# Fetching weight words earlier and chunk inputs later in the first steps of a fused linear-attention and FFN kernel

## The chip, the cores and the metric

The kernel runs on one NeuronCore of a Trainium2 chip. The metric is the device time of one execution in microseconds (us); lower is better. The engines are named as in the profile: PE is the matrix engine (PEld its weight loads), DVE the vector engine, ACT the scalar engine, POOL the GpSimd engine, and SP the engine whose queue issues most of the DMA transfers.

## The reference, cut to what matters

```python
# attention: B=4, H=8, S=768, D=48, all float32
for t in range(S):
    state = alpha[:, :, t, :, None] * state + einsum('bhd,bhe->bhde', k[:, :, t], v[:, :, t])
    y[:, :, t] = einsum('bhd,bhde->bhe', q[:, :, t], state)
# bridge: y (B,H,S,D) -> x (B*S, H*D) = (3072, 384)
# FFN: w1, w2 (384, 1024), w3 (1024, 1024), w_out (1024, 384), all float64 in memory
a = x @ w1
b = x @ w2
h = a * b @ w3
out = h @ w_out          # (3072, 384)
```

The gated recurrence of every head feeds a multiplicative FFN. The FFN weights arrive as float64 words, and the kernel itself turns them into float32.

## The kernel before, in words

**Chunks and steps.** The sequence of each batch is cut into chunks of 128 rows, six to a batch, so there are `N` = 24 chunks over the four batches. The main loop (line 599) runs `n` from 0 to 24; one round is called a step. In step n the kernel computes the score matrices of chunk n (`scores`, PE line 364, masked on DVE line 367), finishes the attention output of chunk n-1 (`attend_state` line 384, `attend` line 390, copied out by ACT line 394), forms the new state (`outer`, line 336) and transposes q and k of chunk n+1 (`transposed`, PE line 324, copied by ACT line 326). It also prepares later chunks: `decayed(n + 2)` (DVE line 302) multiplies k and q by the decay factors, `logs(n + 4)` (ACT line 271) takes logarithms of alpha, and `decays(n + 3)` (PE lines 286 and 289, ACT lines 292 and 293) sums them and takes exponentials. Chunk inputs come by the SP queue: alpha by `load_a` (line 132), k and q by `load_kq` (lines 138 and 139), v by `load_v` (line 144). Each such load is 192 KB in rows of 192 bytes. At the head of step n the kernel before issues v of chunk n+3, alpha of chunk n+5 and k, q of chunk n+4 (`AHEAD` is 4).

**Weight units.** The w1 and w2 matrices are cut into twelve units of 128 x 512 words of 8 bytes (512 KB each). `load_gates` is a generator: its first call issues the transfer (line 192), and four more calls do the conversion. The first of these works out mantissa and exponent (DVE lines 201 and 204, ACT lines 200 and 205), the second combines them (DVE lines 207, 208 and 210), the third makes the rounded high part (ACT line 217), and the fourth makes the low part (DVE line 219). `fetch(ahead)` issues transfers until `ahead` units are under way, and `convert(steps, ahead)` makes so many calls. For the first six units, which hold the columns that the first four tiles of a gate use, the third part of the split comes from two PE matmuls and an ACT copy (`third`, lines 232 to 234).

**Gates.** Three chunks make a group of 384 rows. When a group's three outputs have been written to DRAM (`store`, line 261), `load_x` (line 406) reads them back transposed as `xT`, `split_x` splits them into three parts (ACT line 412, DVE lines 413 and 414), and `gate` multiplies them with w1 and w2. A gate of one tile of columns has two pieces of nine PE matmuls each (line 420); after six of the nine, ACT line 429 scales the partial sum, and DVE line 431 adds the rest. During the main loop the gates of the first tiles fill PE: `run(...)` takes pieces from the deque `fill`, and `pieces` says how many a step takes. Group g begins in step 6 + 4g of the kernel before, and its pieces are taken 3, 3 and 2 in the three following steps.

**After the loop.** The remaining gates are put in a list `todo` (line 668), in which the folding of w3 with w_out is interleaved (`fold`, PE line 522 and line 420 with `w3T`). When the folding is done, its memory is closed, a new pool is opened, and `load_ab` (line 543) and `split_ab` (ACT line 550, DVE lines 551 and 552) bring back the products for the last stage, `project` (line 420 with `w3o`).

**What sets the order.** The order of the instructions on each engine is fixed at build time. The program's order and the calls of `after_marks`, which put instructions behind a named earlier one, decide it. SP issues its transfers in that order as well.

Of the kernel before, what the change touches and what calls it, by code (L numbers as in the profile page):

```python
# [10 lines left out]
FP32 = mybir.dt.float32  # L11
# [5 lines left out]
ALU = mybir.AluOpType  # L17
# [3 lines left out]
P = 4096.0  # L21
# [27 lines left out]
def kernel(  # L49
# [12 lines left out]
    nc = tc.nc  # L62
# [5 lines left out]
    N = B * NCH  # L68
    NP = H // 2
    DP = 64  # L70
    KM = DM // C
    KF = DF // C
# [4 lines left out]
    AHEAD = 4  # L77
# [28 lines left out]
    st, mark = {}, {}  # L106

    def after_marks(*names):
        stack = ExitStack()
        for x in names:  # L110
            stack.enter_context(tc.issue_after(mark[x]))
        return stack
# [12 lines left out]
    def rows(src, n):  # L125
        b, c = divmod(n, NCH)
        return src[b, :, ds(c * C, C), :].rearrange("h p d -> p h d")

    def load_a(n):
        if n < N:  # L130
            st["a", n] = inp.tile([C, H, D], FP32, tag="ac", name="ac")
            nc.sync.dma_start(out=st["a", n], in_=rows(alpha, n))  # L132

    def load_kq(n):
        if n >= N:
            return
        st["kq", n] = inp.tile([C, 2, H, D], FP32, tag="kq", name="kq")
        nc.sync.dma_start(out=st["kq", n][:, 0], in_=rows(k, n))  # L138
        nc.sync.dma_start(out=st["kq", n][:, 1], in_=rows(q, n))  # L139

    def load_v(n):
        if n < N:
            st["v", n] = vs[n % len(vs)]
            nc.sync.dma_start(out=st["v", n][:, :, 0:D], in_=rows(v, n))
# [69 lines left out]
    def load_gates(i, kk, half):  # L214
        w = yield from to_fp32(None, (moe_w1, moe_w2)[i][ds(kk * C, C), ds(half * CW, CW)])
        h, l, m = (w12[half][:, x, i, kk, :] for x in range(3))
        nc.scalar.activation(h, w, AF.Copy, scale=(1.0 - 2.0 ** -13) / P)
        yield
        nc.vector.scalar_tensor_tensor(l, h.bitcast(FP32), -P, w, op0=ALU.mult, op1=ALU.add)
        if half:  # L220
            nc.vector.scalar_tensor_tensor(m, h.bitcast(FP32), P + 1.0, w, op0=ALU.mult, op1=ALU.subtract)
        else:
            thirds.append((m, h, l))

    weights, begun, thirds = deque(), deque(), deque()

    def third(count):

# [7 lines left out]
    def fetch(ahead=3):  # L236
        while weights and len(begun) < ahead:
            begun.append(weights.popleft())
            next(begun[-1])

    def convert(steps, ahead=3):

        for _ in range(steps):
            fetch(ahead)
            if not begun:
                return
            x = begun.popleft()
            try:
                next(x)
                begun.appendleft(x)  # L250
            except StopIteration:
                pass
# [27 lines left out]
    def decays(n):  # L280
        if n >= N:
            return
        lc = bank()[:, 0:DM]
        la = st.pop(("la", n))
        if n < LATE:
            nc.tensor.matmul(lc, sums[:, n % 2].bitcast(FP32), la, start=True, stop=True)  # L286
        else:
            for i in range(2):
                nc.tensor.matmul(lc, sums[:, n % 2], la[:, i], start=(i == 0), stop=(i == 1))  # L289

        e = st["e", n] = work.tile([C, 2, DM], FP32, tag="e", name="e", bufs=3)
        nc.scalar.activation(e[:, 0], lc, AF.Exp, scale=-1.0)
        mark["e", n] = nc.scalar.activation(e[:, 1], lc, AF.Exp).ins  # L293
        if n in ends:
            nc.gpsimd.dma_start(out=ends[n][0:1], in_=e[0:1, 0])
        if n + 1 in ends:
            nc.gpsimd.dma_start(out=ends[n + 1][1:2], in_=e[C - 1:C, 1])
        load_ends(n)
# [109 lines left out]
    def split_x(g, i):  # L408
        x = st.pop(("xT", g))
        t = tr[i].tile([C, 3, KM, TG], FP32R, tag="x3", name="x3")  # L410
        st["x3", g] = t
        nc.scalar.activation(t[:, 0], x, AF.Copy, scale=1.0 - 2.0 ** -13)
        nc.vector.tensor_sub(t[:, 1], x, t[:, 0].bitcast(FP32))
        mark["x3"] = nc.vector.scalar_tensor_tensor(t[:, 2], t[:, 0].bitcast(FP32), -1.0 - 1.0 / P, x,
                                                    op0=ALU.mult, op1=ALU.add).ins
# [73 lines left out]
    def gate(g, f):  # L489
        yield from (late_gate if late else early_gate)(g, f)  # L490
# [71 lines left out]
    fill = deque()  # L562
# [11 lines left out]
    FH = CW // C  # L574
# [9 lines left out]
        logs(1)  # L584
    decays(1)
    fetch(1)
    load_v(1)
    load_kq(2)
    load_a(3)
    decayed(1)  # L590
    load_v(2)
    load_kq(3)
    load_a(4)


    begin = {4 + 4 * g: (g, range(FH if g < 4 else KF)) for g in range(5)}
    loads = {8: 1, 11: 2, 15: 3, 19: 4}

    for n in range(N + 1):
        store()  # L600
        if n in loads:
            load_x(loads[n])
        load_v(n + AHEAD - 1)
        load_a(n + 5)
        load_kq(n + AHEAD)
        if n:
            attend_state(n - 1)
        if n < N:
            scores(n)
        transposed(n + 1)  # L610
        if n - 2 in begin:
            g, tiles = begin[n - 2]
            with after_marks(("ms", n), ("qkT", n + 1)):
                split_x(g, 0)
            fill.extend(gate(g, f) for f in tiles)
        pieces = (0, 3, 3, 2)[(n - 6) % 4] if n > 5 else 0
        if n == 0:
            with after_marks(("qkT", 0)):
                logs(2)
            decays(2)  # L620
            with after_marks(("e", 2)):
                logs(3)
        early, ready = n < 7, len(thirds)
        behind = after_marks(*[("qkT", n + 1)] * (n < N - 1), *[("qk", n + 1)] * early, *["x3"] * (n - 2 in begin))
        if n < N - 2:
            with behind:
                convert(2 if n == 0 else 1, 2 if n == 0 else 3 if n < 8 else 4)
        advance(n)
        if n:
            attend(n - 1)  # L630
        outer(n)
        third(ready)
        run(pieces > 0)
        if early:
            with after_marks(("qkT", n + 1), ("qk", n + 1)):
                convert(1)
        with after_marks(*[("ms", n)] * (n < 3)):
            decayed(n + 2)
        logs(n + 4)
        if n == 4:  # L640
            load_x(0)
        convert(early and n > 2)
        run(pieces > 1)
        decays(n + 3)
        if n < N - 2:
            convert(early or n % 3 == 0, 3 if n < 8 else 4)
        run(pieces > 2)
        if n == N - 3:
            while begun:
                convert(1)  # L650
            weights.extend(load_out(j) for j in range(KF))
            fetch(4)
# [91 lines left out]
```

## Time and profile before

| quantity | value |
|---|---|
| median of three runs | 480.21 us (478.72 to 480.35) |
| profiled execution, own time | 478.61 us |
| span of its instructions | 476.8 us |
| PE busy / weight loads busy | 458.3 us (96%) / 435.2 us (91%) |
| DVE / ACT / POOL busy | 356.3 us (75%) / 282.1 us (59%) / 73.1 us (15%) |
| moved by DMA | 80.29 MB, mean 168 GB/s |
| mean granted PE clock | 0.982 |

The profiled execution took 478.61 us, of which 1.8 us lie outside the span of its instructions; its time is 1.6 us below the median of the three runs. The page cuts the span into 40 equal slices of 11.9 us. A busy PE in it is not a PE at full speed: where the granted clock is half, the same matmuls count about twice the time.

### The profile page before, as it was taken

What the parts mean: (1) busy time and instruction counts of PE and PEld (TensorE: products, weight loads), DVE (VectorE), ACT (ScalarE), POOL (GpSimd) and SP (SyncE); (2) the same over time, 40 slices, a digit from 0 to 9 for tenths busy, and PEclk for the clock granted to TensorE, in tenths of its full rate; (3) what the DMA queues carried; (4) which work ended last, traced back from release to release, by engine and by line L of the source; (5) the groups of instructions that cost most, each with busy time, mean ns of one, the idle gap of its engine ahead of it and who ended that gap; (6) DMA issues with size and microseconds to landing.
All of it is one profiled execution on the core that took longest, in us unless ns stands there. A gap on an engine that the chain in (4) does not pass through costs nothing.

```text
span 476.8 us, 10002 instructions
## 1 busy us (share of the span) xinstructions
PE 458.3 (96%) x3836; PEld 435.2 (91%) x3836; DVE 356.3 (75%) x576; ACT 282.1 (59%) x556; POOL 73.1 (15%) x140
## 2 busy tenths in 40 slices
PE   4879899999999999999999999999999999999996
PEld 2658589899899999999999999999999999999996
DVE  2769888886988988999998888745642876666761
ACT  4667766866758555898876666644545433333330
POOL 3321231112302310212331101202010100000000
PEclk9888889999999999999999999999999999999999
DMA  9999999999999964657775333122105965555511
GB/s 171 178 200 220 241 211 212 229 234 211 197 216 206 210 202 133 200 170 234 242 216 209 109 124 100 50 84 90 44 36 157 261 189 169 164 170 172 177 51 49
DMA packets 153583, 80.29 MB, mean 168 GB/s; under 512 B 104480, under 2 KB 145568, under 8 KB 153536
## 3 DMA queue, kind: packets, MB, share of 16 engines
q1 hardware_dynamic: 148016, 65.22, 56.8%
q0 software_dynamic: 5520, 14.43, 9.5%
q8 instruction: 30, 0.49, 0.5%
q14 instruction: 17, 0.14, 0.1%
HBM read 57.58 MB, written 22.06 MB: 167 GB/s over the span
## 4 chain that ended last, share of the span: by engine, by line
PE 87%; DMA 5%; SPq 3%; DVE 2%; ACT 1%; issue 1%; DVEq 0%; ACTq 0%
PE bank L420 70%; PE bank L364 5%; PE bank L390 4%; DMA raw<-in_moe_w_dram 4%; PE bank L384 2%; PE bank L324 2%; SPq L139 2%; PE bank L336 1%; PE bank L522 1%; PE bank L289 1%; DMA ac<-in_alpha_dram 1%; SPq L138 1%; SPq L132 1%; PE bank L286 1%; DVE ms L367 0%
## 5 line engine op out<-in xcount | busy, mean ns | idle before, releaser
L420 PE MATMUL bank<-x,w 128*128 128x384 f32 x1152 | 210.9, 337 | 0.0
L420 PEld LDWEIGHTS bank<-x,w 128*128 128x128 f32 x1152 | 200.4, 188 | 1.3 <-issue 0.7
L420 PE MATMUL bank<-w3o,ab 128*128 128x384 f32 x576 | 100.2, 336 | 0.0
L420 PEld LDWEIGHTS bank<-w3o,ab 128*128 128x128 f32 x576 | 99.9, 188 | 0.0
L445 ACT ACTIVATE bank<-bank 128x384 f32<-128x384 f32 x98 | 46.7, 477 | 43.6 <-PE bank L420 43.3
L429 ACT ACTIVATE t<-bank 128x384 f32<-128x384 f32 x62 | 30.6, 494 | 62.3 <-PE bank L420 60.1
L495 POOL DMA_DIRECT2D abd<-ab x46 | 26.9, 584 | 132.8 <-DVE ab L481 125.2
L481 DVE TENSOR_TENSOR ab<-bank,r 128x384 f32<-128x384 f32 x45 | 24.9, 552 | 23.4 <-ACT bank L445 18.6
L551 DVE TENSOR_TENSOR ab<-abl,ab 128x1024 fp32r<-128x1024 f32 x24 | 29.4, 1224 | 13.6 <-ACT ab L550 13.5
L550 ACT ACTIVATE ab<-abl 128x1024 fp32r<-128x1024 f32 x24 | 25.5, 1061 | 20.9 <-PE bank L420 19.2
L326 ACT COPY qkT<-bank 128x512 f32<-128x512 f32 x48 | 26.1, 591 | 19.0 <-PE bank L324 19.0
L367 DVE TENSOR_TENSOR ms<-bank,keep 128x512 int32<-128x512 int32 x48 | 31.4, 683 | 7.8 <-PE bank L364 7.8
L420 PE MATMUL bank<-wo,w3T 128*128 128x384 f32 x192 | 35.9, 334 | 0.0
L420 PEld LDWEIGHTS bank<-wo,w3T 128*128 128x128 f32 x192 | 33.5, 188 | 0.0
L364 PEld LDWEIGHTS bank<-qkT 48*128 48x128 f32 x384 | 25.7, 204 | 7.0 <-issue 4.2
L431 DVE SCALAR_TENSOR_TENSOR o<-bank,t 128x384 f32<-128x384 f32 x24 | 13.4, 557 | 24.0 <-issue 15.6
L364 PE MATMUL bank<-qkT 48*128 48x128 f32 x384 | 30.7, 304 | 0.4 <-ACT qkT L326 0.4
L552 DVE SCALAR_TENSOR_TENSOR ab<-ab,abl 128x1024 fp32r<-128x1024 f32 x24 | 29.2, 1217 | 0.0
L302 DVE TENSOR_TENSOR qk<-kq,e 128x768 f32<-128x768 f32 x24 | 23.0, 958 | 8.2 <-ACT e L293 8.1
L390 PE MATMUL bank<-ms,v 128*64 128x128 f32 x384 | 28.3, 293 | 0.0
L205 ACT ACTIVATE power<-power,rebias 128x512 uint32<-128x512 uint32 (+1 forms) x36 | 25.1, 701 | 4.1 <-DVE power L204 3.8
L200 ACT ACTIVATE rest<-raw 128x512 f32<-128x512 uint32 (+1 forms) x36 | 23.3, 650 | 7.1 <-DMA raw<-in_moe_w_dram 7.1
(80 smaller groups left out, 573.3 us busy)
## 6 DMA issues: line engine op xcount, KB each, us to landing
raw<-in_moe_w_dram SPq DMA_DIRECT2D x28, 512.0 KB, 5.2
abl<-abd SPq DMA_DIRECT2D x24, 512.0 KB, 4.6
abd<-ab POOLq DMA_DIRECT2D x46, 192.0 KB, 3.1
xT<-xd POOLq DMA_DIRECT2D x9, 576.0 KB, 4.5
ac<-in_alpha_dram SPq DMA_DIRECT2D x24, 192.0 KB, 4.7
kq<-in_k_dram SPq DMA_DIRECT2D x24, 192.0 KB, 5.4
kq<-in_q_dram SPq DMA_DIRECT2D x24, 192.0 KB, 4.4
v<-in_v_dram SPq DMA_DIRECT2D x24, 192.0 KB, 5.0
```

Of the source, the lines that this page charges most:

```text
L205: nc.scalar.activation(power, power, AF.Relu, scale=2.0 ** 23, bias=rebias)
L326: mark["qkT", n] = nc.scalar.copy(qkT[:, :, :, ds(DP * half, DP)], tp[half]).ins
L364: nc.tensor.matmul(sc[i][:, j, :], qkT[r, 0, j, :], qkT[r, 1, j, :], start=True, stop=True)
L367: masked = nc.vector.tensor_tensor(ms[:, i].bitcast(I32), sc[i].bitcast(I32), keep_bc, op=ALU.bitwise_and)
L390: nc.tensor.matmul(to, vc[:, 2 * j + i, :], ms[:, i, j, :], start=(n % NCH == 0 and j % HP == 0), stop=(j % HP == HP - 1), skip_group_chec ...
L420: nc.tensor.matmul(p, w[part][i], x[part][i], start=start and part == parts[0] and i == 0, stop=stop and part == parts[-1] and i == n - 1, ...
L429: nc.scalar.activation(t, p1, AF.Copy, scale=(1.0 + 1.0 / P) * scale)
L445: nc.scalar.activation(p, p, AF.Copy, scale=1.0 + 1.0 / P)
L495: (nc.gpsimd if late else nc.sync).dma_start(out=abd[g][:, f, :], in_=ab)
L550: nc.scalar.activation(t[:, 0], ab, AF.Copy, scale=1.0 - 2.0 ** -13)
L551: nc.vector.tensor_sub(t[:, 1], ab, t[:, 0].bitcast(FP32))
L552: nc.vector.scalar_tensor_tensor(t[:, 2], t[:, 0].bitcast(FP32), -1.0 - 1.0 / P, ab, op0=ALU.mult, op1=ALU.add)
```

## The change: its parts and the diff

Before the loop, k, q and v of one chunk less are loaded, alpha of chunk 3 moves ahead of k and q of chunk 2, and a second weight unit is fetched. In steps 0 to 6, k and q are issued three chunks ahead and v two; step 6 issues two chunks of them, and from then on the distance is the old one. The number of units under way is written out per step in `raws`, and a `fetch` stands ahead of the k, q, v loads in steps 0 to 3. One more `convert` call is made in steps 1 and 2, and none of the extra ones in step 6, so that all 24 calls for the first six units are made by the end of step 5. The first group's `split_x` moves from step 6 to the end of step 5, behind the last low part of a unit (`mark["l"]`). Every later group begins a step sooner, and the pieces are taken 3, 3, 2, 0 beginning in step 6 rather than 0, 3, 3, 2. The `load_x` calls keep their steps. In the static order of the changed program one gate less is left for `todo`: 36 matmuls instead of 54 stand between the last fold's `w3T` matmuls and the first `w3o` matmuls.

```diff
--- before.py
+++ after.py
@@ -216,13 +216,14 @@
         h, l, m = (w12[half][:, x, i, kk, :] for x in range(3))
         nc.scalar.activation(h, w, AF.Copy, scale=(1.0 - 2.0 ** -13) / P)
         yield
-        nc.vector.scalar_tensor_tensor(l, h.bitcast(FP32), -P, w, op0=ALU.mult, op1=ALU.add)
+        mark["l"] = nc.vector.scalar_tensor_tensor(l, h.bitcast(FP32), -P, w, op0=ALU.mult, op1=ALU.add).ins
+        done.append((i, kk, half))
         if half:
             nc.vector.scalar_tensor_tensor(m, h.bitcast(FP32), P + 1.0, w, op0=ALU.mult, op1=ALU.subtract)
         else:
             thirds.append((m, h, l))
 
-    weights, begun, thirds = deque(), deque(), deque()
+    weights, begun, thirds, done = deque(), deque(), deque(), []
 
     def third(count):
 
@@ -584,47 +585,51 @@
         logs(1)
     decays(1)
     fetch(1)
+    load_a(3)
+    load_kq(2)
     load_v(1)
-    load_kq(2)
-    load_a(3)
     decayed(1)
-    load_v(2)
-    load_kq(3)
+    fetch(2)
     load_a(4)
 
 
-    begin = {4 + 4 * g: (g, range(FH if g < 4 else KF)) for g in range(5)}
+    FIRST = 6
+    begin = {FIRST - 3 + 4 * g: (g, range(FH if g < 4 else KF)) for g in range(5)}
     loads = {8: 1, 11: 2, 15: 3, 19: 4}
 
     for n in range(N + 1):
         store()
         if n in loads:
             load_x(loads[n])
-        load_v(n + AHEAD - 1)
         load_a(n + 5)
-        load_kq(n + AHEAD)
+        raws = (3, 3, 3, 3, 2, 2, 3, 3)[n] if n < 8 else 4
+        if n < FIRST - 2:
+            fetch(raws)
+        for m in (n + 3,) * (n <= FIRST) + (n + 4,) * (n >= FIRST):
+            load_kq(m)
+            load_v(m - 1)
         if n:
             attend_state(n - 1)
         if n < N:
             scores(n)
         transposed(n + 1)
-        if n - 2 in begin:
+        if n - 2 in begin and n > FIRST:
             g, tiles = begin[n - 2]
             with after_marks(("ms", n), ("qkT", n + 1)):
                 split_x(g, 0)
             fill.extend(gate(g, f) for f in tiles)
-        pieces = (0, 3, 3, 2)[(n - 6) % 4] if n > 5 else 0
+        pieces = (3, 3, 2, 0)[(n - FIRST) % 4] if n >= FIRST else 0
         if n == 0:
             with after_marks(("qkT", 0)):
                 logs(2)
             decays(2)
             with after_marks(("e", 2)):
                 logs(3)
-        early, ready = n < 7, len(thirds)
-        behind = after_marks(*[("qkT", n + 1)] * (n < N - 1), *[("qk", n + 1)] * early, *["x3"] * (n - 2 in begin))
+        early, ready = n < FIRST, len(thirds)
+        behind = after_marks(*[("qkT", n + 1)] * (n < N - 1), *[("qk", n + 1)] * early, *["x3"] * (n - 2 in begin and n > FIRST))
         if n < N - 2:
             with behind:
-                convert(2 if n == 0 else 1, 2 if n == 0 else 3 if n < 8 else 4)
+                convert(2 if n == 0 else 1, raws)
         advance(n)
         if n:
             attend(n - 1)
@@ -633,17 +638,23 @@
         run(pieces > 0)
         if early:
             with after_marks(("qkT", n + 1), ("qk", n + 1)):
-                convert(1)
+                convert(1, raws)
         with after_marks(*[("ms", n)] * (n < 3)):
             decayed(n + 2)
         logs(n + 4)
         if n == 4:
             load_x(0)
-        convert(early and n > 2)
+        convert(early and n > 0, raws)
         run(pieces > 1)
         decays(n + 3)
         if n < N - 2:
-            convert(early or n % 3 == 0, 3 if n < 8 else 4)
+            convert(early or n % 3 == 0, raws)
+        if n == FIRST - 1:
+            assert len(done) == 2 * KM
+            g, tiles = begin[n - 2]
+            with after_marks("l"):
+                split_x(g, 0)
+            fill.extend(gate(g, f) for f in tiles)
         run(pieces > 2)
         if n == N - 3:
             while begun:
```

## Prediction

> **What bounds the kernel now.** I began with the page's totals and its 40 slices, then read the chain of waits, the windows and the timeline of the first 90 us, and last the timeline where the final stage begins. By "step n is at t" I mean that its first matmuls on PE begin at t.
>
> ```profile
> PE 458.3 (96%) x3836; PEld 435.2 (91%) x3836; DVE 356.3 (75%) x576; ACT 282.1 (59%) x556; POOL 73.1 (15%) x140
> ...
> PE   4879899999999999999999999999999999999996
> ...
> PEclk9888889999999999999999999999999999999999
> DMA  9999999999999964657775333122105965555511
> ```
>
> The reader is to see two regimes. PE is full from the sixth slice to the end, so from there only an idle PE gap costs or gains time. In the first five slices PE has gaps and a reduced clock, while DMA is at 9 throughout. The chain of waits says who holds PE there (start, length, what):
>
> ```profile
> 23.79 5.58 DMA raw<-in_moe_w_dram
> ...
> 31.52 6.32 DMA raw<-in_moe_w_dram
> ...
> 46.79 5.69 DMA raw<-in_moe_w_dram
> ...
> 56.77 1.65 PE bank L286 x2
> 58.42 2.01 PE bank L364 x16
> ...
> 79.69 0.60 PE bank L384 x16
> ```
>
> So until about 57 us the chain runs through transfers, and afterwards through PE. These windows are step 6, step 7 before its first gate, and the rest of step 7 (columns: stretch, its length, busy PE, PEld, DVE, ACT, POOL, then clock, DMA share, GB/s):
>
> ```profile
> 50.50:58.35 7.85, 5.87 (x75) 3.78 (x69) 6.47 (x12) 5.39 (x12) 1.89 (x3) 0.88 0.99 237
> 58.35:64.27 5.92, 5.92 (x67) 5.66 (x67) 4.29 (x6) 3.63 (x6) 1.31 (x1) 0.58 1.23 230
> 64.27:70.80 6.53, 5.52 (x34) 4.94 (x36) 5.54 (x12) 4.95 (x12) 1.87 (x6) 1.00 0.99 222
> ```
>
> PE has about 2 us idle in step 6, a clock of 0.58 in the base work of step 7, and again 1 us idle after the first gates. That is what an earlier gate could use. The start of the gates itself:
>
> ```profile
> 59.27 1.16 ACT L412 ACTIVATE x<-xT 128x1152 fp32r<-128x1152 f32 x1
> ...
> 61.67 1.35 DVE L413 TENSOR_TENSOR x<-xT,x 128x1152 fp32r<-128x1152 f32 x1
> ...
> 64.27 1.91 PE L420 MATMUL bank<-x,w 128*128 128x384 f32 x10
> ```
>
> L412 begins 0.02 us after the trace's landing of xT at 59.25; L413 waits until DVE is free. Last, the start of the final stage:
>
> ```profile
> 362.66 9.52 PE L420 MATMUL bank<-x,w 128*128 128x384 f32 x54
> ...
> 367.35 1.06 ACT L550 ACTIVATE ab<-abl 128x1024 fp32r<-128x1024 f32 x1 [0.90 <-DMA abl<-abd]
> ...
> 368.44 1.23 DVE L551 TENSOR_TENSOR ab<-abl,ab 128x1024 fp32r<-128x1024 f32 x1 [3.58 <-ACT ab L550]
> ...
> 372.02 4.32 PE L420 MATMUL bank<-w3o,ab 128*128 128x384 f32 x24
> ```
>
> 54 gate matmuls hide the first load and split of `abl`: the split is usable at 369.67, PE wants it at 372.02.
>
> **What the Trainium skill says.** "DMA: Bandwidth & Descriptors", section "Issuing engines are not separate DMA queues": all transfers share the same 16 engines and interleave. The trace agrees: the DMA share is 0.91 or more in every 10 us up to 170 us, so reordering transfers moves landings about but frees nothing. "TensorE: Matmul & The Clock Gate", section "Part 1: The HAM clock gate": after an idle window of about 3.4 us PE falls to half clock, and a busy window brings it back. The trace agrees in its steps: the clock is half from 32.64 to 39.46 and from 56.53 to 63.36, two windows of 3.41 us each, and the 16 matmuls of line 364 take 2.08 us at 58.35 against 1.16 at 50.55. It differs in one thing: here a window with about 2 us of work in 3.41 (53.1 to 56.5) was enough to drop the clock. The same section calls ACT and DVE strict FIFO; L413 above shows it, held by two masks although ACT was done at 60.43.
>
> **The change, part by part.** *The transfers.* Up to 60 us landings follow the order of issue, about four loads behind it. In the changed order, what SP issues up to q of chunk 7 is 32 small loads, 6 raw units and 3 store pairs. In the kernel before exactly that many, with one v for one alpha, end with the second store of chunk 2, which landed at 53.10. So q of chunk 7 lands at 53.1 (before: 49.85), the sixth unit about 46 (52.48), and then one v (0.93, the step from that store to the next v) and xT (1.98, the step from q of chunk 8 to xT) give xT at 56.0 (59.25). Six weight units gain over 6 us, but x gains only 3.2, since it stands behind the small loads that remain.
>
> *The chain to the first gate.* On DVE `decayed(7)` now stands ahead of the last low part and the split; on ACT the split stands behind qkT of chunk 7. So: q at 53.1, L302 0.95, L324 about 0.5 to 1.1 by clock, two L326 together 1.07: 55.8 to 56.2. Then xT at 56.0 is there, L412 1.16, L413 1.35: the first gate can start at G = 58.7. DVE isn't late: at 0.6 us from start to start of its 0.68 us operations a step is 3.1 of conversion, 1.2 of masks, 0.95 and 0.3, so 5.5, where the transfers of a step take 6.9 (v of chunk 6 at 47.16, of chunk 7 at 54.03). The two added conversions in steps 1 and 2 hide there. If the cover were gone, they would cost their own 1.2 us.
>
> *What PE then does.* Both kernels have the same work done when step 10 begins, at 87.03 in the trace (the two halves have eight pieces each by then). The changed one needs after G: step 6, 27 matmuls at 0.18 (3.34 for 18) and L286 0.85, 5.7; step 7, base 1.09+0.50+1.02+0.45, L289 0.35, 27 matmuls 4.9, 8.3; step 8 with 18 matmuls, 7.34 as step 9 now; step 9 without gates, 4.2 as step 10 now. Sum 25.6, so step 10 at 84.3, a gain of 2.7 at full clock. But PE is idle while it waits for q of chunk 7 and again from about 56.7 to 58.7, and its work between 53 and 58.7 is some 2.2 us; by what 53.1 to 56.5 did in the trace it starts the gates at half clock. With the same windows that lasts to 63.36, 4.7 us at half speed, a loss of 2.3. Left: 0.4. Bounds: no loss at all, or 3.4 if two whole windows are cold.
>
> *Later steps.* Chunk loads regain the old distance in step 6, and the queue is as far as before, plus two stores of products that come a step sooner. xT of group 1, landed 83.51, comes about 1.3 later by those; its split is needed at 90 (step 10 at 86.6 plus 3.1 to 3.7 of base), and 84.8+1.16+1.35+1.35 is 88.7. Cost 0, with 1.3 of slack. The later units 7 to 12 are fetched later; their columns are wanted only at the end of part one, so 0. PE's idle times of 0.23 in 90 to 100 and 0.19 in 120 to 130 come after gate-free steps whose alpha landed late (93.70 used at 94.42; 122.89 used at 123.27); these steps move a chunk earlier, and alpha moves ahead of v in the queue, so I count 0.4 gained, with bounds 0.4 either way.
>
> *The final stage.* With 36 matmuls instead of 54, at 9.36/54 = 0.173, the cover is 6.2 us, to 368.9. The split is usable at 369.67, as SP's loads hang on the last `w3T` matmul. Cost 0.8, bounds 0 (loads land sooner with less beside them) and 1.5.
>
> Sum: +0.4 +0.4 -0.8 = 0. Against its own time the profiled execution stays at 478.6; the median before is 1.6 above that, and I carry the zero over to the median: **480.2**.
>
> **The rivals.** *Faster.* The clock is full when the gates begin, because PE's waits are shorter or fall across two windows, or G is up to 1 us sooner. For: the trace kept full clock from 39.5 to 56.5, and the 27 matmuls are then worth all of 2.7. Against: the wait for the split lies in front of them, as above. Gain 2.3 to 3.3: 476.9 to 477.9.
>
> *Slower.* Transfers just in time: k and q of each chunk now land in the step that uses them, so one late transfer stops DVE at L302, and behind it in its queue stand the rest of a unit's conversion, the masks that PE's line 390 waits for, and the split. Place: `decayed(7)`. Price: one for one. From G = 58.7 on each us is lost; past 61.1 the kernel is over 2.4 slower. For: landings in the trace slip by 2.3 (31.91 to 34.22) and 2.8 (42.92 to 45.76), which slack of 4.9 and 1.4 in q hid in part. Against: such slips are already in the 53.1. One more of 2.4 to 2.8, with up to 0.7 more in the final stage (its upper bound): 482.6 to 483.7.
>
> *It doesn't do what it says.* Six units are converted by step 5 in program order in any case; but if x alone sets G, the weights' 6 us buy nothing, and the result is the same zero. It is inside the main case.
>
> **How the numbers follow.** 0.5% is 2.4 us, about what a measurement of this kernel can tell from no change. Main case (including the third rival) 0.56, its own range 478.2 to 482.2 (clock loss 1 us either way, final stage and idle times 1 us either way). Faster 0.24, slower 0.20. The range is 476.7 to 482.9, which leaves out the far half of either rival.
>
> **What would show it.** Right: xT of group 0 lands near 56, L412 follows line 326 at about 56, the first L420 at 58 to 60 with matmuls at twice their time and a half clock to 62 or beyond; step 10 near 86.6; a PE gap of under 1 us ahead of the first `w3o` matmul. Wrong: gates that begin at full clock or before 57.5 (faster), L302 of chunk 7 after 55.5 (slower), or PE idle above 1 us in steps 9 to 11, where xT of group 1 would be late.

## The result: the same time, and the profile after

| | before | changed |
|---|---|---|
| median, 14 runs each, same chip | 479.71 us (478.50 to 481.18) | 479.68 us (477.75 to 481.87) |
| profiled execution, own time / span | 478.61 / 476.8 us | 479.55 / 477.8 us |
| mean granted PE clock | 0.982 | 0.988 |

The ratio of the changed kernel to the one before is 0.9996, with a 95% interval of 0.998 to 1.0012. A second group of runs on another chip, 22 of the changed kernel, gave 1.0017 (1.0004 to 1.0029). No difference of 0.5% is there. Below, this second pair of profiled executions is called the second profile of each kernel (477.23 us before, 479.04 changed), the other the first. In the changed kernel lines after 219 stand one further down: L302 is now L303, L326 is L327, L412 to L414 are L413 to L415, and L420 is L421.

From the page of the changed kernel, the totals and the slices:

```profile
PE 457.0 (96%) x3836; PEld 432.6 (91%) x3836; DVE 358.6 (75%) x578; ACT 279.5 (58%) x555; POOL 73.4 (15%) x139
...
PE   4798799999999999999999999999999999999996
...
PEclk9979899999999999999999999999999999999999
DMA  9999999999999954467776542213012985555511
```

The picture is that of before: PE has gaps in the first five slices and is full afterwards, and DMA is at 9 up to the fifteenth slice. The chain of waits of the changed kernel (start, length, what):

```profile
14.23 5.51 DMA raw<-in_moe_w_dram
...
54.66 0.96 DVE qk L303
...
57.61 1.07 ACT x L413
58.70 1.36 DVE x L414
60.06 1.28 DVE x L415
61.47 2.33 PE bank L421 x12
...
145.57 4.09 DMA ac<-in_alpha_dram
...
150.11 0.58 ACT qkT L327
150.73 2.38 PE bank L421 x12
```

Before, the chain passed from transfers to PE at 57 us. Now the split of x stands in it, all three instructions, up to 61.47, and it falls back to an alpha transfer at 145.57. The timeline shows the start of the gates (columns: start, length, engine, line, operation, tiles; in brackets the idle time ahead of it and what ended it):

```profile
54.66 0.95 DVE L303 TENSOR_TENSOR qk<-kq,e 128x768 f32<-128x768 f32 x1
...
56.53 1.08 ACT L327 COPY qkT<-bank 128x512 f32<-128x512 f32 x2 [2.03 <-PE bank L325]
57.49 1.17 ACT L413 ACTIVATE x<-xT 128x1152 fp32r<-128x1152 f32 x1
58.70 1.36 DVE L414 TENSOR_TENSOR x<-xT,x 128x1152 fp32r<-128x1152 f32 x1 [1.22 <-ACT x L413]
58.72 0.79 PE L421 MATMUL bank<-x,w 128*128 128x384 f32 x3 [1.00 <-ACT x L413]
...
60.11 0.80 PE L421 MATMUL bank<-x,w 128*128 128x384 f32 x3 [0.60 <-DVE x L414]
61.47 2.33 PE L421 MATMUL bank<-x,w 128*128 128x384 f32 x12 [0.56 <-DVE x L415]
```

The first gate begins at 58.72 instead of 64.27, but PE stops three times on the way, once for each part of x, for 2.16 us together. The second profile of the kernel before shows how little the first one fixes this moment:

```profile
58.03 1.17 ACT L412 ACTIVATE x<-xT 128x1152 fp32r<-128x1152 f32 x1 [0.78 <-DMA xT<-xd]
...
60.22 1.21 PE L420 MATMUL bank<-x,w 128*128 128x384 f32 x6
```

There the gates of the unchanged kernel begin at 60.22, and it reaches L364 of step 10 at 84.29 rather than 87.56. The table follows the four profiles, and three experiments, through the same marks. "Half clock" lists the stretches of half PE clock later than 40 us and before 100; step 10 and step 22 are taken at their first matmul of scores.

| kernel | xT landed | first gate | step 10 | from step 10 to 22 | from 22 to the end | half clock |
|---|---|---|---|---|---|---|
| before, first | 59.25 | 64.27 | 87.56 | 86.83 | 302.42 | 56.5 to 63.4 |
| before, second | 58.01 | 60.22 | 84.29 | 88.54 | 302.62 | none |
| changed, first | 56.16 | 58.72 | 86.41 | 88.45 | 302.92 | 49.5 to 52.9 |
| changed, second | 54.40 | 59.31 | 88.30 | 86.04 | 302.92 | 41.0 to 44.4, 61.5 to 64.9 |
| loads only | 56.85 | 68.51 | 91.69 | 85.72 | 302.42 | 40.2 to 47.0, 64.1 to 70.9 |
| gates only | 60.84 | 62.25 | 91.41 | 86.13 | 302.88 | 60.8 to 67.7 |
| x other queue, alpha first | 55.38 | 59.00 | 85.36 | 86.68 | 302.94 | 40.8 to 47.7 |

In the first pair the changed kernel is 1.15 us ahead at step 10; in the second pair it is 4.01 behind. In both pairs the kernel that was ahead gives back 1.6 to 2.5 us by step 22. The first profile of the changed kernel has two stops of PE in that stretch, of 1.4 us together, and the second has none, so that they don't belong to the change as such. What follows had to separate the parts of the change, since two profiles of one kernel differ by more than the change moves.

### The profile page after: what moved, and what is told of

Read it like the earlier page. It is cut to its first block, busy times and chain, and to the rows that moved or that the text cites. A ratio compares the mean times of both kernels' runs of the same rounds, so it can differ in the third digit from the quotient of the medians.

```text
span 477.8 us, 10015 instructions
## 1 busy us (share of the span) xinstructions
PE 457.0 (96%) x3836; PEld 432.6 (91%) x3836; DVE 358.6 (75%) x578; ACT 279.5 (58%) x555; POOL 73.4 (15%) x139
## 4 chain that ended last, share of the span: by engine, by line
PE 85%; DVE 5%; DMA 3%; SPq 3%; ACT 2%; issue 1%; DVEq 0%; ACTq 0%
PE bank L421 69%; PE bank L365 4%; PE bank L391 4%; PE bank L385 2%; PE bank L325 2%; PE bank L523 1%; DMA xd<-x 1%; PE bank L337 1%; DMA raw<-in_moe_w_dram 1%; SPq L139 1%; DVE ms L368 1%; DMA ac<-in_alpha_dram 1%; PE bank L290 1%; DVE qk L303 1%; ACT qkT L327 1%
## 5 line engine op out<-in xcount | busy, mean ns | idle before, releaser
L421 PE MATMUL bank<-x,w 128*128 128x384 f32 x1152 | 212.9, 339 | 3.1 <-ACT x L413 1.0
L421 PEld LDWEIGHTS bank<-x,w 128*128 128x128 f32 x1152 | 199.9, 188 | 6.8 <-ACT x L413 1.4
L421 PE MATMUL bank<-w3o,ab 128*128 128x384 f32 x576 | 100.2, 337 | 0.0
L421 PEld LDWEIGHTS bank<-w3o,ab 128*128 128x128 f32 x576 | 99.9, 188 | 0.0
L446 ACT ACTIVATE bank<-bank 128x384 f32<-128x384 f32 x96 | 45.7, 477 | 41.8 <-PE bank L421 41.5
L496 POOL DMA_DIRECT2D abd<-ab x45 | 25.5, 567 | 145.0 <-DVE ab L482 126.2
L552 DVE TENSOR_TENSOR ab<-abl,ab 128x1024 fp32r<-128x1024 f32 x24 | 29.4, 1225 | 12.6 <-ACT ab L551 12.5
L327 ACT COPY qkT<-bank 128x512 f32<-128x512 f32 x48 | 25.8, 589 | 19.8 <-PE bank L325 19.8
L421 PE MATMUL bank<-wo,w3T 128*128 128x384 f32 x192 | 35.9, 335 | 0.0
L421 PEld LDWEIGHTS bank<-wo,w3T 128*128 128x128 f32 x192 | 33.5, 188 | 0.0
L368 DVE TENSOR_TENSOR ms<-bank,keep 128x512 int32<-128x512 int32 x48 | 31.3, 682 | 0.8 <-PE bank L365 0.8
L432 DVE SCALAR_TENSOR_TENSOR r<-bank,t 128x384 f32<-128x384 f32 x40 | 22.1, 554 | 13.0 <-ACT t L430 10.6
L303 DVE TENSOR_TENSOR qk<-kq,e 128x768 f32<-128x768 f32 x24 | 22.9, 953 | 8.5 <-ACT e L294 8.4
L391 PE MATMUL bank<-ms,v 128*64 128x128 f32 x384 | 27.1, 285 | 0.0
```

The source lines that it names most:

```text
L303: mark["qk", n] = nc.vector.tensor_mul(qks[n % 3][:, :, :, 0:D], st.pop(("kq", n)), st.pop(("e", n)).rearrange("p i (h d) -> p i h d", h=H ...
L327: mark["qkT", n] = nc.scalar.copy(qkT[:, :, :, ds(DP * half, DP)], tp[half]).ins
L368: masked = nc.vector.tensor_tensor(ms[:, i].bitcast(I32), sc[i].bitcast(I32), keep_bc, op=ALU.bitwise_and)
L391: nc.tensor.matmul(to, vc[:, 2 * j + i, :], ms[:, i, j, :], start=(n % NCH == 0 and j % HP == 0), stop=(j % HP == HP - 1), skip_group_chec ...
L421: nc.tensor.matmul(p, w[part][i], x[part][i], start=start and part == parts[0] and i == 0, stop=stop and part == parts[-1] and i == n - 1, ...
L432: nc.vector.scalar_tensor_tensor(to, p2, scale, t, op0=ALU.mult, op1=ALU.add)
```

## The experiments

Each ratio is to runs of the kernel before on the same chip in the same group; their medians were 478.40 (loads only, alpha first, fewer v), 478.14 (gates only, x other queue) and 478.11 us (the rest). The theory was that the change is two moves which need each other: the new order of the loads brings x early, and the sooner gates use it, so that the net is what is left of a gain near 55 us after clock and later waits. The rival was that one move pays by itself and the other costs, or that neither matters. The third part of the change, the earlier conversions, stays in both of the first two experiments and was not tested alone.

### The order of the loads alone

```diff
-    begin = {FIRST - 3 + 4 * g: ...
+    begin = {FIRST - 2 + 4 * g: ...
-        pieces = (3, 3, 2, 0)[(n - FIRST) % 4] if n >= FIRST else 0
+        pieces = (0, 3, 3, 2)[(n - FIRST) % 4] if n >= FIRST else 0
...
-        if n == FIRST - 1:
-            ...
-                split_x(g, 0)
```

> The changed kernel with its new order of loads and conversions, but with every group's gates in their old steps. In the two profiles the changed kernel is 1.15 us ahead of the kernel before when step 10 begins, with equal PE work done. If the earlier gates bring that lead, this kernel has none of it: step 7 may begin a little sooner than at 58.35, the gates wait for step 7, and the time is 480 to 481. Rival: the lead comes from the order of loads (six units done sooner), then step 10 begins near 86 here too and the time is about that of the changed kernel or below, 479 to 480.

Measured: 481.25 us, ratio 1.0074 (1.0056 to 1.0092), so slower by 2.9 us. From its timeline:

```profile
60.02 1.36 DVE L414 TENSOR_TENSOR x<-xT,x 128x1152 fp32r<-128x1152 f32 x1 [1.22 <-ACT x L413]
61.30 1.35 DVE L415 SCALAR_TENSOR_TENSOR x<-x,xT 128x1152 fp32r<-128x1152 f32 x1
...
63.63 0.95 DVE L303 TENSOR_TENSOR qk<-kq,e 128x768 f32<-128x768 f32 x1
...
64.73 1.12 PE L325 MATMUL bank<-ident,qk 64*128 64x64 f32 x16 [3.93 <-DVE qk L303]
...
68.51 1.97 PE L421 MATMUL bank<-x,w 128*128 128x384 f32 x5
```

k and q of chunk 8, now fetched a chunk later, had landed at 59.99. But L303, which multiplies them, stands on DVE behind both of its parts of the split and a mask, and PE has no gates yet to pass the time: it is idle for 3.93 us and then runs at half clock. In the first profile of the kernel before, the same multiplication stands ahead of DVE's parts of the split, the first of which begins at 61.67:

```profile
57.88 0.95 DVE L302 TENSOR_TENSOR qk<-kq,e 128x768 f32<-128x768 f32 x1
```

So the stop comes from the place on DVE that goes with this order of loads: L303 begins 3.6 us after its data are there. How the time would be with the old place on DVE was not run. With the sooner gates the same moment of the changed kernel is filled with gate matmuls. As built, the new order of loads is a loss by itself.

### The sooner gates alone

```diff
-    load_a(3); load_kq(2); load_v(1); decayed(1); fetch(2); load_a(4)
+    load_v(1); load_kq(2); load_a(3); decayed(1); load_v(2); load_kq(3); load_a(4)
...
+        load_v(n + AHEAD - 1)
         load_a(n + 5)
+        load_kq(n + AHEAD)
+        raws = 2 if n == 0 else 3 if n < 8 else 4
-        (the fetch ahead of the loads, and the loop that issues load_kq(m), load_v(m - 1))
```

> The changed kernel's conversions and earlier gates with the old order of loads. In the kernel before the sixth unit lands at 52.5 and xT at 59.3, so with the old loads the four calls for that unit stand in step 5 behind 52.5, and the split behind both. Theory: the order of loads is what makes the earlier gates possible, about 3.2 us of xT's landing; here the gates start near 62.5 instead of 58.7 and the time is 2 to 3.5 us above the changed kernel. Rival: the order of loads buys nothing (the split is held by DVE's queue); then it is within 0.7 us of the changed kernel.

Measured: 482.76 us, ratio 1.0103 (1.008 to 1.0126), the slowest version of all. From its timeline:

```profile
61.05 1.15 ACT L413 ACTIVATE x<-xT 128x1152 fp32r<-128x1152 f32 x1
...
62.25 1.33 PE L421 MATMUL bank<-x,w 128*128 128x384 f32 x3 [4.32 <-ACT x L413]
...
63.92 4.78 PE L421 MATMUL bank<-x,w 128*128 128x384 f32 x15 [0.34 <-DVE x L414]
```

xT lands at 60.84 in the old order of loads. PE stands still for 4.32 us, and the 15 matmuls that follow take 4.78 us. At full clock 18 of them take 3.41, so 15 would take about 2.8. Against the changed kernel of the same group (478.75 us) the new order of loads is worth 4.0 us once the gates are sooner.

Together the two runs settle the main point. One half costs 2.9 us, the other 4.6, both together about nothing. The halves don't add: the sooner gates fill the stop of 3.93 us that the new loads leave, and the new loads shorten the wait of 4.32 us for x that the sooner gates meet.

### Fewer v loads: is the beginning bound by transfers?

In both kernels the loads of v for chunks 8 to 23 are left out, so these chunks use what lies in their buffers:

```diff
-            nc.sync.dma_start(out=st["v", n][:, :, 0:D], in_=rows(v, n))
+            if n < 8:
+                nc.sync.dma_start(out=st["v", n][:, :, 0:D], in_=rows(v, n))
```

The kernel before with it:

> The kernel before without the v loads of chunks 8 to 23 (old v data is used in their place), which takes 16 loads of about 1.1 us off the DMA engines from step 5 on. PE bounds the kernel before from 60 us on but for gaps of 0.4 us in all, so the time should fall by 0.4 to 1 us only, by every theory.

The changed kernel with it:

> The changed kernel without the v loads of chunks 8 to 23 (old v data is used in their place). If the lead of 1.15 us at step 10 is given back because transfers are late from step 12 on, this kernel keeps it: it is 1 to 2 us faster than the kernel before without the same loads, and step 22 begins about 1 us sooner instead of 0.47 later. Rival: the lead is lost for another reason (gates among attention work run slower, a lucky clock in one profile); then both kernels without these loads take the same time within 0.5 us.

Measured: 475.27 us for the kernel before, ratio 0.9953 (0.9932 to 0.9974); 478.48 for the changed one, ratio 1.0008 (0.9995 to 1.002). This is not what I expected: the kernel before gains 3.1 us and the changed one about nothing. The gain does not come from an xT that is no longer behind v. In the kernel before, SP (SPq is its queue) issues v of chunk 8 only after xT:

```profile
53.93 0.92 SPq L406 DMA_DIRECT2D xT<-xd  x1
...
56.60 0.56 SPq L144 DMA_DIRECT2D v<-in_v_dram  x1
```

In the changed kernel it comes later still, at 62.99. So nothing that happens in the first 55 us can be due to the missing loads; that the profile of the kernel before with fewer v has no half clock there is the scatter of executions once more. The difference is seen later. With fewer v the kernel before reaches step 10 at 83.68 and needs 86.31 us to step 22, with no stop of PE; its second profile with all loads reaches step 10 at 84.29 and needs 88.54, with three stops of 1.39 us together. The changed kernel with fewer v reaches step 10 at 86.95 and needs 86.02, as its second profile did (86.04). So the profiles suggest that a kernel which is early at step 10 loses time to the transfers that follow, and that one which is late has none to lose there. Whether the beginning itself is bound by transfers these two runs can't tell, and 0.8 us of the difference between 88.54 and 86.31 is not seen as stops.

### Alpha ahead of the other transfers of a step

The first profile of the changed kernel had lost 1.6 us between steps 10 and 22. The list of waits for ACT from 85 to 176 us names alpha (L272) and the stores of the attention output (L395; columns: who waited for what, total us, times, longest):

```profile
ACT la L272 <- DMA ac<-in_alpha_dram: 7.7, 5, 3.7
...
ACT x L395 <- DMA xd<-x: 5.9, 3, 3.1
```

Most of it is idle time that costs nothing, but each of the two reaches PE once. Its timeline:

```profile
123.21 0.65 ACT L395 COPY x<-bank 128x256 f32<-128x256 f32 x2 [3.09 <-DMA xd<-x]
...
125.89 0.71 PE L325 MATMUL bank<-ident,qk 64*128 64x64 f32 x15 [0.42 <-ACT e L294]
...
149.68 0.52 ACT L272 ACTIVATE la<-ac 128x384 f32<-128x384 f32 x1 [1.94 <-DMA ac<-in_alpha_dram]
150.11 1.06 ACT L327 COPY qkT<-bank 128x512 f32<-128x512 f32 x2
150.73 2.38 PE L421 MATMUL bank<-x,w 128*128 128x384 f32 x12 [0.95 <-ACT qkT L327]
```

The first stop of PE follows a wait for a store: ACT works without a pause from 123.21 up to L294. The second follows a wait for alpha: L327 doesn't need alpha; it stands behind L272 on ACT, and PE waits for L327. The edit issues alpha first from step 7 on:

```diff
+        if n > 6:
+            load_a(n + 5)
         store()
         ...
-        load_a(n + 5)
+        if n <= 6:
+            load_a(n + 5)
```

> The changed kernel with the alpha load of steps 7 and later issued at the head of the step, ahead of the two stores and the xT load. In the changed kernel alpha of chunks 16 to 23 is used 0.02 to 0.3 us after its landing, ACT waits there up to 1.9 us, and PE has gaps of 0.42 at 125.9 and 0.95 at 150.7. If late alpha is what gives the lead back, these gaps go and the time falls by 1 to 1.5 us against the changed kernel. Rival: the queue is simply full and whatever is moved ahead delays the stores, on which ACT line 395 waits (3.1 us at 123.2); then other gaps take their place and the time stays within 0.5 us.

Measured: 479.81 us, ratio 1.0039 (1.0021 to 1.0058). In its profile no wait for alpha is left in that stretch and step 10 to 22 takes 86.58, but that execution, at 477.68, was the fastest of its ten. By the median nothing is gained, and if anything some is lost, which fits neither expectation. The second profile of the changed kernel suggests why: it waits for alpha once, for 1.1 us, with 86.04 from step 10 to 22. A kernel that reaches step 10 later finds its alpha there. In the version with the loads alone (step 10 at 91.69) alpha of chunks 14 to 19 had landed 1.9 to 3.8 us before its use, in the second profile of the kernel before (84.29) five of these six only 0.02 to 0.1. In these profiles the wait takes back a lead, and where there is none it is absent.

### x on POOL's queue and its split ahead

In the changed kernel the split stands behind the last low part (`mark["l"]`), and ACT reaches L413 only after L327. In the second profile xT lay there from 54.40, and L413 began at 58.08. Here the load of xT is issued by POOL, and the split is put behind an earlier mark:

```diff
+        if n == FIRST - 1:
+            with after_marks(("ms", n), ("qkT", n + 1)):
+                split_x(0, 0)
...
-            load_x(0)
+            load_x(0, nc.gpsimd)
...
-            with after_marks("l"):
-                split_x(g, 0)
```

> The changed kernel with the first xT load issued on POOL's queue, so that it doesn't stand behind the loads on SP, and with the first split placed in step 5 ahead of the transposed copies of chunk 7. In the changed kernel PE waits 2.2 us for the parts of that split (gaps of 1.00, 0.60 and 0.56 from 58.7 to 61.5). If x alone sets the start of the gates, the split ends by 58.8, step 7 begins 1.2 to 2 us sooner and the time falls by as much, to a ratio of 0.996 to 0.998. Rival: q of chunk 7 and the last conversion, which stand ahead on DVE, hold the gates just as long; then step 7 moves by less than 0.5 us and the time stays.

Measured: 477.45 us, ratio 0.9989 (0.9976 to 1.0003); the changed kernel of the same group had 478.75, so 1.3 us less; the ratio lies between the two expectations. From its timeline:

```profile
54.58 1.21 ACT L413 ACTIVATE x<-xT 128x1152 fp32r<-128x1152 f32 x1
...
55.45 0.71 PE L325 MATMUL bank<-ident,qk 64*128 64x64 f32 x16 [1.36 <-DVE qk L303]
...
55.82 1.35 DVE L414 TENSOR_TENSOR x<-xT,x 128x1152 fp32r<-128x1152 f32 x1
...
57.25 3.50 PE L421 MATMUL bank<-x,w 128*128 128x384 f32 x17
```

xT landed at 54.24 and L413 follows at once. The three stops of PE at the first gate are gone: after the wait for L303 there is one of 0.11 us. PE reaches step 10 at 83.64, the earliest of the versions with their full loads, but then takes 88.15 to step 22, with waits for alpha again (3.2 us on ACT). Part of the 83.64 belongs to this execution: the next version, which is the same up to step 7, has 85.36. And which of the two edits brings the gain was not separated: SP too had xT there at 54.40 in the second profile of the changed kernel, against 54.24 by POOL here, so the sooner split may be all of it.

### Both of these

```diff
+ the two edits above together: alpha first from step 7, x on POOL with the split ahead
```

> The first xT on POOL's queue with the earlier split, and alpha at the head of steps 7 and later, both in the changed kernel. Alone, the first put step 10 at 83.64 instead of 86.4 to 88.3, but steps 10 to 22 took 88.14 us instead of 86.0, so that the ratio was 0.9989. In the profile with alpha first, steps 10 to 22 took 86.6. If late alpha is what gives the lead back, steps 10 to 22 take at most 87 here and the ratio is 0.995 to 0.997. Rival: the transfers as a whole are late, whatever is ahead; then steps 10 to 22 stay at 88 and the ratio at 0.998 to 1.000.

Measured: 476.61 us (475.13 to 477.35), ratio 0.9967 (0.9954 to 0.998), the only complete version faster than both kernels. Its list of waits for ACT from 85 to 176 us begins

```profile
ACT t L430 <- PE bank L421: 13.0, 14, 1.3
ACT qkT L327 <- PE bank L325: 11.2, 10, 2.1
```

and holds no transfer: ACT now waits for PE. From step 10 to 22 it takes 86.68, as expected. That alpha first keeps the lead is not shown by this: the profile reaches step 22 at 172.04, the version before at 171.79, having begun step 10 sooner, and the intervals of the two ratios overlap. What is shown is that the edits together make the changed kernel faster. The gain is 1.5 us on a median of 478.11, under the 0.5% that the prediction took as its bound.

### The products on POOL's queue too

On top of the version before, `store_ab` always uses POOL's queue:

```diff
-            (nc.gpsimd if late else nc.sync).dma_start(out=abd[g][:, f, :], in_=ab)
+            nc.gpsimd.dma_start(out=abd[g][:, f, :], in_=ab)
```

> As the kernel with xT on the other queue and alpha first, and the stores of the gates' products inside the loop on POOL's queue too (19 stores of 192 KB), so that loads on SP no longer stand behind a store that waits for DVE. If SP's order is what makes the loads late, steps 10 to 22 fall to 86 to 86.5 and the ratio is 0.994 to 0.997. Rival: the DMA engines themselves are the limit; then it is within 0.1% of the kernel without this move.

Measured: 478.96 us, ratio 1.0021 (1.0007 to 1.0035); 2.3 us are lost against the version without it, which neither expectation had. From its timeline:

```profile
121.39 0.52 ACT L272 ACTIVATE la<-ac 128x384 f32<-128x384 f32 x1 [4.72 <-DMA ac<-in_alpha_dram]
...
121.82 1.05 ACT L327 COPY qkT<-bank 128x512 f32<-128x512 f32 x2
...
122.44 0.79 PE L421 MATMUL bank<-x,w 128*128 128x384 f32 x3 [1.83 <-ACT qkT L327]
```

The old pattern is back, alpha late, L327 behind it, PE idle for 1.83 us, and then a half clock from 123.3 to 126.7. Emptying SP's queue didn't bring alpha sooner.

### The same two ideas in the kernel before

The load of xT on POOL and alpha first, with the gates, the place of the split and the chunk loads of the kernel before:

```diff
-            load_x(0)
+            load_x(0, nc.gpsimd)
+        if n > 6:
+            load_a(n + 5)
```

> The kernel before (old order of loads, old steps of the gates) with the first xT on POOL's queue and alpha at the head of steps 7 and later. In its two profiles xT lands 0.5 to 1.2 us ahead of its use, and the gates begin only after step 7's base work; so xT sooner should bring at most 0.5 us, and alpha first some 0.4 to 1.4 us of gaps in steps 10 to 15: ratio 0.997 to 1.000. If it equals the changed kernel with the same two edits, the change itself brings nothing with them either; if it is 1 us or more above, the change is what lets an earlier xT pay.

Measured: 481.75 us, ratio 1.0073 (1.0049 to 1.0096), where I had expected no such loss. From its timeline:

```profile
57.76 0.79 POOL L406 DMA_DIRECT2D xT<-xd  x1
...
64.83 1.16 ACT L412 ACTIVATE x<-xT 128x1152 fp32r<-128x1152 f32 x1 [5.08 <-DMA xT<-xd]
...
67.08 1.05 PE L336 MATMUL bank<-v,qk 128*64 128x48 f32 x16 [3.47 <-ACT qkT L326]
...
69.07 3.13 PE L420 MATMUL bank<-x,w 128*128 128x384 f32 x13
```

POOL issues xT only at 57.76, where SP did so at 53.9, behind an instruction of its own (L310) that had waited 4.59 us for a transfer, and xT lands at 64.81 rather than 59.25. L412 waits for it at the head of ACT's queue, the copy of q and k behind it waits too, and PE with it. So these edits as they stand don't speed up the kernel before. What an xT that really lands sooner would bring there, the run can't tell, since it came later.

### PE kept busy at the first gates

Six matmuls whose result nothing reads are put into steps 5 and 6 of the changed kernel:

```diff
+        if n in (5, 6):
+            p = bank()
+            for i in range(6):
+                nc.tensor.matmul(p, signs[:, 0], w12[0][:, 0, 0, 0, :], start=(i == 0), stop=(i == 5))
```

> The changed kernel with six more matmuls of 128 x 512, whose sum is never read, after third in step 5 and again in step 6 (1.3 us each at full clock), where PE waits for q of chunk 7 and for the split. Theory of the prediction: the waits drop the clock just ahead of the gates, which costs 2.3 us; then these keep it full at the gates in every execution and the time falls by 1 to 2 us against the changed kernel (ratio 0.998 to 1.000). Rival: the clock is mostly full there anyway (three of four profiles of this order of gates), so that the time changes by less than 0.5 us, or rises by the length of the added matmuls where they delay the chain.

Measured: 477.40 us, ratio 0.9989 (0.9978 to 1.0). From its timeline:

```profile
53.29 0.95 DVE L303 TENSOR_TENSOR qk<-kq,e 128x768 f32<-128x768 f32 x1
...
58.02 1.56 PE L641 MATMUL bank<-w,signs 128*128 128x512 f32 x6
59.41 1.21 PE L421 MATMUL bank<-x,w 128*128 128x384 f32 x6
```

The ratio is lower than the changed kernel's 1.0017 on another chip, though not clearly lower than its 0.9996 in the first group, and the added matmuls (1.56 us for six) do fill the time ahead of the first gate. But the run doesn't isolate the clock. The added instructions also shifted the static order, so that L303 of chunk 7 came at 53.29 rather than 54.66, and the stretches of half clock (25.8 to 32.6 and 49.7 to 53.1) are nearly those of the changed kernel's first profile. How much of it the clock is worth stays open.

## Why the prediction was right, step by step

**The time.** 480.2 was forecast and 479.68 measured. The net of zero is right, and the two single parts show that it is a net of large terms and not of small ones. But the terms differ from what was forecast: it had +0.4 us up to step 10, +0.4 later and -0.8 in the last stage, and the first pair of profiles has +1.2, -1.6 and -0.5. That their sum comes near zero all the same is in part luck. One of its own signs of being wrong, gates that begin at full clock, came true in both profiles; a half clock during the gates comes only in the second, from 61.5 to 64.9.

**Transfers.** The sixth unit was put at about 46 and landed at 44.39; xT at 56.0, and it landed at 56.16. That last agreement is luck: q of chunk 7 was put at 53.1 and landed at 51.13, two microseconds too late in the working, and the step from q to v, put at 0.93, took 3.46. The third rival, that x alone sets the first gate, is excluded for the changed kernel: in its second profile xT landed 1.8 us sooner, and the gate began 0.6 later.

**The chain to the first gate.** G was forecast at 58.7 and came at 58.72 and 59.31. That agreement is luck, for two errors cancel. The forecast let the chain start with the landing of q; in the trace q had been there for 3.5 us when L303 began at 54.66, held up on DVE behind a part of the conversion (L207 to L210) and a mask (L368) that waited 0.83 us for PE. So ACT's part of the split began at 57.49, 1.3 us later than forecast. But the forecast also put DVE's first part of the split, 1.35 us, ahead of the first gate, and the first matmul needs ACT's part alone. The order of instructions on DVE and ACT sets G: in the second profile xT lay there for 3.7 us when L413 began, and the run with the split ahead agrees.

**PE from G to step 10.** Steps 7, 8 and 9 were forecast at 8.3, 7.34 and 4.2; the timeline has 8.31, 7.33 and 4.21. Step 6 was forecast at 5.7 and took 7.24. The working let all of its gates run on from G; it left out that the fourth matmul needs L414 and the seventh L415, whose waits of 0.60 and 0.56 make most of the 1.5.

**The clock.** A loss of 2.3 was forecast, with bounds from 0 to 3.4. The first profile has none at this place; in the second, 12 matmuls from 62.06 take 3.64 us against 2.33, so it costs 1.3. This term was mis-sized. What makes it uncertain is in the table: the kernel before as well has a half clock from 56.5 to 63.4 in one profile and none there in the other. The forecast took one profile of before as its base, and that was the unfavourable one, by 3.3 us at step 10. That the clock at this place alone moves the median was not isolated.

**Step 10.** 86.6 was forecast, counted from its first matmul on PE; that is at 85.81 by the timeline, where the kernel before has 86.96 (the forecast used 87.03, from the chain of waits). The gates gained 1.2 there in the first pair of profiles where 0.4 was forecast.

**Later steps.** A gain of 0.4 was forecast; the first pair shows a loss of 1.6, the second a gain of 2.5. The working treated the later transfers as fixed in place, ahead of their use. They are not: when PE is early, alpha and the stores are late by comparison, and ACT's queue carries the wait to PE. The stops of 0.95 at 150.73, behind alpha, and 0.42 at 125.89, behind a store, make 1.4 us, where the kernel before has 0.4 in all. For the rest of the difference between profiles no gap is seen.

**The final stage.** A cost of 0.8 was forecast for the missing cover, with bounds 0 and 1.5. The lower bound held. From the timeline of the changed kernel:

```profile
366.80 6.40 PE L421 MATMUL bank<-x,w 128*128 128x384 f32 x36
...
371.49 1.06 ACT L551 ACTIVATE ab<-abl 128x1024 fp32r<-128x1024 f32 x1 [0.90 <-DMA abl<-abd]
...
372.59 1.23 DVE L552 TENSOR_TENSOR ab<-abl,ab 128x1024 fp32r<-128x1024 f32 x1 [3.58 <-ACT ab L551]
...
373.04 4.32 PE L421 MATMUL bank<-w3o,ab 128*128 128x384 f32 x24
```

The `w3o` matmuls begin at 373.04, before L552 ends at 373.82, with no gap on PE. The mistake was to count to the end of the split's second part; the first matmuls need ACT's part alone, which is done at 372.55. Still, every profile with the sooner gates takes 302.67 to 302.94 us from step 22 to the end, every one with the old steps 302.42 to 302.62. About 0.4 us are lost there in another way. One gate more runs in the loop, and in the first profile of the changed kernel the gate matmuls of steps 22 to 24 follow each other by 0.177 to 0.191 us, against 0.173 at the end of the gates; for 18 of them that is an estimated 0.1 to 0.3 us. The remainder is open.

**The rivals.** "Slower" named a late transfer that stops DVE at L302, in `decayed(7)`. It didn't come, since q was early. A stop of PE at the next such place, `decayed(8)`, costs 3.93 us in the version with the loads alone, but by the reverse: there the data were in time, and the split ahead in DVE's queue held them up. "Faster" asked for gates at full clock; the first profile has that, and the kernel still wasn't faster, because 1.2 of the gain went into the parts of the split, 1.4 into the stops behind alpha and a store and 0.5 into the last stretch.

## What to carry to other kernels

Two moves of one change can each be a loss and together break even, because each removes the idle time that the other makes; measure the halves before keeping or dropping either. When an instruction has to wait for a transfer, look at what stands behind it in its engine's queue: here a copy that needed nothing of alpha made PE wait. In the profiles, alpha issued first and fewer loads both took that stop away; whether the time falls with it seems to depend on whether there is a lead to keep. Take at least two profiles of the base kernel before working out a gain near a moment where a transfer and a clock change meet.

## What the runs showed of the hardware

- The stretches of half clock come and go between executions of one program: the kernel before has 32.6 to 39.5 and 56.5 to 63.4 in one profile, 33.1 to 36.5 and no later one in the other, in multiples of about 3.4 us. The Trainium skill's "TensorE: Matmul & The Clock Gate", section "Part 1: The HAM clock gate", ties them to idle windows of that length. The traces agree in the length, but the windows ahead were not idle: in the first profile of the kernel before PE was busy for 1.88 of the 3.41 us ahead of the drop at 56.53. That landings differing by 1 to 2 us decide whether PE has enough work in a window is my reading, not shown. Mean clock and time go together only loosely: in the three groups of the experiments, eight executions of the kernel before with 0.981 took 478.40 to 479.77 us, and thirty with 0.996 took 475.32 to 480.05.
- A transfer moved to POOL's queue can be later by far. xT moved so landed at 54.24 and 55.38 in the changed kernel, but at 64.81 in the kernel before, where POOL came to it only at 57.76. The skill's "DMA: Bandwidth & Descriptors", section "Issuing engines are not separate DMA queues", says that another engine saves only the issue time; here the place in the other engine's program mattered as well: of the 5.6 us lost, 3.8 lie in the later issue. That POOL's queue brings xT sooner than SP's is not shown: SP landed it at 54.40 and 56.16 in the changed kernel.
